# A chunked-attention and channel-mixer kernel on one core: two late tiles turned on TensorE, one batch's halving done in the lead-in, and the slot lists set anew

## The chip, the cores and the metric

The kernel runs on one core of one Trainium2 chip. A core has five engines that run side by side, each taking its own instructions strictly in order: TensorE (PE, with its weight loads as PEld), VectorE (DVE), ScalarE (ACT), GpSimd (POOL) and SyncE (SP, which here only issues transfers). The metric is the device time of one execution in microseconds, from the first to the last instruction and a little around it; lower is better.

## The reference

```python
# attention, within chunks of 64 positions, for 8 batches, 8 heads, 576 positions, head size 64
scores = scale * np.matmul(q_c, k_c.transpose(0, 1, 2, 4, 3))
attn = softmax(scores)                       # row maximum taken off, exp, divided by the sum + 1e-9
x = matmul(attn, v_c)                        # then laid out as [batch, 576, 512]
# mixer
h = x.transpose(0, 2, 1) @ U @ V             # rank 32, along the positions
u = x + h.transpose(0, 2, 1)
out = u + np.maximum(u @ w_ch1, 0.0) @ w_ch2 # 512 -> 2048 -> 512
```

q, k and v are float32; U, V, w_ch1 and w_ch2 are float64 and are rounded to float32 pairs on the chip. The two large products are done in three passes each (high times high, high times low, low times high), which is what makes TensorE the busiest engine.

## The kernel before, in words

The 8 x 576 positions are cut into 36 tiles of 128, T0 to T35; two batches make a pair of nine tiles (T0 to T8, T9 to T17, T18 to T26, T27 to T35). In names, the first number is the pair and the second the tile in it, so `es_8` of pair 1 belongs to T17 and `us_0` to T9. The tiles are taken in ten groups (`GROUPS`, line 55): groups 0 to 2 have three tiles, the others four, but for the last with three. For a group, each of 16 rounds f does `hidden` (line 759: 12 multiplications of the group's turned x+u with one slice of w_ch1 into a PSUM bank), `relu_high` on ACT (line 777) and `relu_low` on DVE (line 782), and `project_out` (line 789: three multiplications for each tile of the group, two with the high half of the relu and one with the low half). A round's `project_out` stands one round later in the program.

Groups 0 and 1 and everything before them, the lead-in, are put in order by a small planner (lines 129 to 211). From group 2 on the order is written by hand in `LISTS` (line 958): one string for a group, each word a step and the slot at which it is recorded. A round has one slot more than the group has tiles. What the loop records there is placed on each engine by the compiler's own scheduler, so order may shift by a few rows. The words: `m` loads a tile's q, k and v; `t` turns q and k; `s` takes scores and exp and sends the result through DRAM; `q` turns the result that came back; `a` multiplies with v; `p` and `y` take x times U; `l` computes x+u; `f` and `u` bring it into its turned form; `w` splits it into a high (ACT, line 735) and a low half (DVE, line 739); `r` fetches x+u again for the end.

From pair 1 on no operand is turned on TensorE. q and k are first halved: `halve` (line 390) copies one batch's q or k within DRAM so that 32 columns stand together; eight such transfers make a batch. Those of batches 2 and 3 are issued by SP in the lead-in (line 889), those of batches 4 to 7 by POOL, one in each of nine of a group's 16 rounds (line 1001), each not before a given `hidden` has run. A tile's x+u goes the same way: `put_u` (line 720) writes it to DRAM with four transfers on SP, `fetch_u` (line 723) reads it back turned by blocks, and `square_u` (line 728) turns the blocks of 32 on DVE. Only pair 0 turns x+u on TensorE (`transposed`, line 714). The columns that a group multiplies are complete only when all its tiles have been split, so the last tiles of a group are wanted before the first `hidden` of that group: T9 to T12 before group 3, T13 to T16 before group 4.

Of the kernel before, what the change touches and what calls it, by code (L numbers as in the profile page):

```python
# [11 lines left out]
F32 = mybir.dt.float32  # L12
# [10 lines left out]
def kernel(  # L23
# [11 lines left out]
    nc = tc.nc  # L35
    B, H, S, D = q.shape
# [3 lines left out]
    DF, DM = moe_w_ch2.shape[0], moe_w_ch1.shape[0]  # L40
    P = 128
# [14 lines left out]
    GROUPS += [[13, 14, 15, 16], [19, 20, 17, 18], [21, 22, 23, 24], [27, 28, 25, 26], [29, 30, 31, 32], [35, 33, 34]]  # L56
    PLACES = [0, 3, 0, 2, 0, 2, 0, 2, 0, 3]
    LATE = {2: [12], 3: [15, 16], 4: [19, 20], 5: [23, 24], 6: [27, 28], 7: [31, 32], 8: [35]}
    BLOCKS = [(hp, e, c) for hp in range(HP) for e in range(2) for c in range(2)]
    NPAIR = B // 2  # L60
    SCALE = 1.0 / float(D) ** 0.5
# [7 lines left out]
    dram = ctx.enter_context(tc.tile_pool(name="dram", bufs=1, space=bass.MemoryType.DRAM))  # L69
# [60 lines left out]
    rank = [0]  # L130
# [252 lines left out]
    x_of = {}  # L383
    y_of = {}
    rest = {}
# [17 lines left out]
    def halvings(b):  # L403
        return [lambda w=w: halve(b, *w) for w in [(z, e, g) for z in range(2) for e in range(2) for g in range(2)]]
# [288 lines left out]
    def mix_ops(pr, t, x, ys, after=None, first=None):  # L693
        n = f"{pr}_{t}"
        st = {}
        T = pr * NT + t
# [17 lines left out]
        def transposed():  # L714
            x = x_of[pr, t]
            st["t"] = pt = bank("ut_" + n)
            for cc in range(NCC):
                nc.tensor.transpose(pt[:, cc * P : (cc + 1) * P], x[:, cc * P : (cc + 1) * P], ident)

        def put_u():  # L720
            st["kept"] = put(x_of[pr, t], "us_" + n, by_channel=True)

        def fetch_u():
            st["us"] = fetch(st["kept"], slot(("us", "uT")[T % 2], F32, "us_" + n, (P, P // SQ, P)))
            rest[pr, t] = dram.tile([P, DM], F32, name="rest_" + n)
            nc.gpsimd.dma_start(rest[pr, t], x_of[pr, t])  # L726

        def square_u():
            uT = st["t"] = slot("eT", F32, "uT_" + n)
# [13 lines left out]
        ad = Op("DVE", 0.69, add, lr, free="bank")  # L743
        if (pr, t) == (0, 0):
            Op("PE", 0.01, end_filling, lr, free="bank")
        if pr > 0:
            pu = Op("SP", 2.0, put_u, ad, lat=2.0)
            fe = Op("SP", 2.0, fetch_u, pu, take="us", lat=2.0)
            tr = Op("DVE", 0.71, square_u, fe, take="uT", free="us")
            hi = Op("ACT", 0.59, high, tr, take="" if j else "ut")  # L750
            lo = Op("DVE", 0.69, low, hi, free="uT")
            return [[lr, ad, pu], [fe], [tr], [hi, lo]]
        tr = Op("PE", 0.55, transposed, ad, take="bank")
        hi = Op("ACT", 0.59, high, tr, first, take="" if j else "ut")
        lo = Op("DVE", 0.69, low, hi, free="bank")
# [131 lines left out]
    prev = None  # L887
    blocks = 0
    second = halvings(2) + halvings(3)
    gates = dict(zip(GATES, range(len(GATES))))  # L890
    for g, f0, f1 in STRETCHES:
        for f in range(f0, f1):
            rank[0] = BASE
            prev = block_ops(g, f, f == 0, f == NF - 1, [*w_done[f], *mixed[g]], prev)
            blocks += 1
            if (g, f) == (0, NF - 1):
                last = prev
            if blocks >= HALVES_FROM and second:
                rank[0] = 0
                Op("SP", 0.6, second.pop(0), prev[0], lat=3.0)  # L900
            if blocks in gates:
                rank[0] = 0
                attention_ops(1, gates[blocks], prev[0])
# [23 lines left out]


    assert not second
    to_halve = [w for b in range(4, B) for w in halvings(b)]  # L930
    pend = None

    def flush(j):
# [20 lines left out]
    def do(group):  # L954
# [1 line left out]
            (o.run if isinstance(o, Op) else o)()  # L956

    LISTS = (
# [8 lines left out]
    )  # L967
# [22 lines left out]
    for g, words in enumerate(LISTS, 2):  # L990
        words = words.split()
        slots = 0
        asked = [z.split("@")[0] for z in words]
        late = [z for T in LATE.get(g, []) for z in (f"u{T}", f"w{T}") if z not in asked]
        width = len(GROUPS[g])
        last = g == len(GROUPS) - 1
        for f in range(NF):
            ps = hidden(g, f)
            hh = relu_high(g, f, ps)
            hs = hh, relu_low(g, f, ps, hh)  # L1000
            if (f % 2 or f == 8) and to_halve:
                to_halve.pop(0)()
            for j in range(width + 1):
                while words and int(words[0].split("@")[1]) <= slots:
                    go(words.pop(0).split("@")[0])
                slots += 1
                if f == NF - 1 and j > 0 and late:
                    go(late.pop(0))
                flush(j)
            pend = g, f, hs  # L1010
        assert not words and not late
        if not last:
            for j in range(width):
                flush(j)
            pend = None
# [34 lines left out]
```

## Time and profile before

| | us |
|---|---|
| median of 3 executions | 959.55 (958.25 to 961.33) |
| profiled execution, whole | 957.67 |
| its span, first to last instruction | 955.9 |
| PE busy | 926.7 |
| DVE, ACT, POOL busy | 485.8, 207.5, 235.9 |

How to read the rows: a line of the timeline gives the start from the beginning of the span, the time taken, the engine, the source line, the operation and its tiles (result on the left of the arrow), how many instructions were merged, and in square brackets how long the engine had been idle before and what ended that wait. For transfers issued by SP or POOL the time is that of issuing, not of the transfer.

### The profile page before, as it was taken

What the parts mean: (1) busy time and instruction counts of PE and PEld (TensorE: products, weight loads), DVE (VectorE), ACT (ScalarE), POOL (GpSimd) and SP (SyncE); (2) the same over time, 40 slices, a digit from 0 to 9 for tenths busy, and PEclk for the clock granted to TensorE, in tenths of its full rate; (3) what the DMA queues carried; (4) which work ended last, traced back from release to release, by engine and by line L of the source; (5) the groups of instructions that cost most, each with busy time, mean ns of one, the idle gap of its engine ahead of it and who ended that gap; (6) DMA issues with size and microseconds to landing.
All of it is one profiled execution on the core that took longest, in us unless ns stands there. A gap on an engine that the chain in (4) does not pass through costs nothing.

```text
span 955.9 us, 15482 instructions
## 1 busy us (share of the span) xinstructions
PE 926.7 (97%) x6258; PEld 761.9 (80%) x6258; DVE 485.8 (51%) x891; ACT 207.5 (22%) x347; POOL 235.9 (25%) x314
## 2 busy tenths in 40 slices
PE   7789999999989999999999999999999999999998
PEld 4559899878877787777777878778778888888997
DVE  6789999975446435643455453553355224211211
ACT  5434333322112121112121211112111111111110
POOL 5410000015645345355344421221211001000000
PEclk9999999999999999999999999999999999999999
DMA  9980698445686446755396454431525035200100
GB/s 216 220 247 1 141 193 167 127 144 129 125 184 165 94 103 145 214 135 127 70 235 158 87 128 134 136 97 57 154 90 143 1 88 143 56 1 1 45 1 33
DMA packets 174103, 113.14 MB, mean 118 GB/s; under 512 B 125872, under 2 KB 149424, under 8 KB 174032
## 3 DMA queue, kind: packets, MB, share of 16 engines
q1 hardware_dynamic: 156256, 66.49, 28.8%
q0 software_dynamic: 17168, 45.52, 20.0%
q8 instruction: 49, 0.80, 0.4%
q14 instruction: 22, 0.18, 0.1%
q10 hardware_dynamic: 608, 0.15, 0.1%
HBM read 80.92 MB, written 44.83 MB: 132 GB/s over the span
## 4 chain that ended last, share of the span: by engine, by line
PE 84%; DMA 8%; DVE 3%; SPq 2%; issue 2%; ACT 1%; POOL 0%; DVEq 0%; ACTq 0%; POOLq 0%
PE o L796 38%; PE h L768 38%; PE av L563 2%; DMA qkv<-in_k_dram 2%; PE sc L515 2%; DMA es_4d<-ex 1%; DMA us_6d<-x 1%; SPq L432 1%; PE u L706 1%; PE y L663 1%; SPq L462 1%; PE y L662 1%; DMA es<-es_4d 1%; DMA us<-us_0d 1%; PE y L669 1%
## 5 line engine op out<-in xcount | busy, mean ns | idle before, releaser
L796 PE MATMUL o<-w,hbuf 128*128 128x512 f32 x1728 | 435.6, 395 | 4.0 <-ACT hbuf L779 4.0
L768 PE MATMUL h<-uth,w 128*128 128x512 f32 (+1 forms) x1280 | 390.2, 370 | 2.0 <-DVE ex L536 1.6
L796 PEld LDWEIGHTS o<-w,hbuf 128*128 128x128 f32 x1728 | 321.5, 188 | 71.8 <-ACT hbuf L779 5.1
L768 PEld LDWEIGHTS h<-uth,w 128*128 128x128 f32 x1280 | 237.9, 188 | 36.4 <-issue 2.0
L768 PE MATMUL h<-utl,w 128*128 128x512 f32 (+1 forms) x640 | 236.1, 369 | 1.3 <-DVE utl L739 1.3
L784 DVE SCALAR_TENSOR_TENSOR hbuf<-h,hbuf 128x512 fp32r<-128x512 f32 (+1 forms) x160 | 100.7, 630 | 209.1 <-ACT hbuf L779 208.3
L779 ACT ACTIVATE hbuf<-h 128x512 fp32r<-128x512 f32 (+1 forms) x160 | 88.8, 556 | 486.0 <-PE h L768 484.4
L768 PEld LDWEIGHTS h<-utl,w 128*128 128x128 f32 x640 | 120.4, 188 | 18.5 <-DVE utl L739 1.6
L446 POOL DMA_DIRECT2D vn<-in_v_dram x96 | 59.8, 632 | 8.0 <-issue 8.0
L421 POOL MEMSET vn<- 128x8 f32 x27 | 3.1, 116 | 209.5 <-DVE w L359 141.8
L425 POOL DMA_DIRECT2D qn<-halfq x24 | 21.5, 895 | 131.5 <-DVE kT L471 123.6
L396 POOL DMA_DIRECT2D halfq<-in_q_dram x16 | 40.7, 2544 | 46.6 <-PE h L768 38.7
L471 DVE STREAM_TRANSPOSE uT<-us 128x512 f32<-128x512 f32 x27 | 29.5, 1092 | 42.7 <-DMA us<-us_0d 10.7
L471 DVE STREAM_TRANSPOSE eT<-es 128x512 f32<-128x512 f32 x27 | 29.1, 1078 | 36.0 <-PE h L768 8.7
L396 POOL DMA_DIRECT2D halfk<-in_k_dram x16 | 40.7, 2546 | 21.5 <-PE h L768 11.3
L544 ACT ACTIVATE ex<-ex 128x512 f32<-128x512 f32 x36 | 22.8, 633 | 92.2 <-DVE ex L536 85.9
L471 DVE STREAM_TRANSPOSE qT<-qn 128x512 f32<-128x512 f32 x27 | 19.2, 712 | 42.2 <-PE h L768 39.0
L726 POOL DMA_DIRECT2D rest<-x x27 | 18.0, 668 | 73.3 <-DVE x L712 72.3
L655 DVE TENSOR_TENSOR xl<-x,xh 128x512 fp32r<-128x512 f32 x30 | 20.6, 686 | 28.6 <-PE y L663 28.4
L529 DVE TENSOR_REDUCE mx<-sc 128x4 f32<-128x256 f32 x72 | 28.1, 412 | 12.3 <-PE sc L515 12.0
L712 DVE TENSOR_TENSOR x<-u,x 128x512 f32<-128x512 f32 x36 | 24.0, 681 | 14.6 <-PE u L706 14.4
L563 PEld LDWEIGHTS av<-vn,eT 64*64 64x64 f32 x864 | 17.8, 133 | 17.0 <-issue 17.0
(95 smaller groups left out, 650.4 us busy)
## 6 DMA issues: line engine op xcount, KB each, us to landing
wraw<-in_moe_w_ch_dram SPq DMA_DIRECT2D x32, 512.0 KB, 6.3
rest<-x POOLq DMA_DIRECT2D x27, 256.0 KB, 3.7
rest<-rest POOLq DMA_DIRECT2D x27, 256.0 KB, 4.7
out_dram<-rest SPq DMA_DIRECT2D x27, 256.0 KB, 2.0
vn<-in_v_dram POOLq DMA_DIRECT2D x96, 64.0 KB, 2.5
qn<-halfq POOLq DMA_DIRECT2D x24, 256.0 KB, 3.9
kn<-halfk POOLq DMA_DIRECT2D x24, 256.0 KB, 3.9
halfq<-in_q_dram POOLq DMA_DIRECT2D x16, 288.0 KB, 7.4
```

What stands on the lines that cost most here:

```text
L396: moved = queue.dma_start(halves[pr, z][odd * n : (odd + 1) * n, 2 * e + g].rearrange("n s (h i) -> n s h i", i=SQ), (q, k)[z][b, e * HP : ...
L425: queue.dma_start(dst.rearrange("p (n a) c -> p n a c", n=2), halves[pr, z][2 * t : 2 * t + 2].rearrange("n x (j a) c -> (x j) n a c", a=2),)
L446: d = queue.dma_start(vn[e * C : (e + 1) * C, c, :, 0:D], v[b, heads(pr, t, e), s0 : s0 + C, :].rearrange("h s d -> s h d"),)
L471: turned = nc.vector.transpose(dst, src)
L529: nc.vector.reduce_max(mx, st["sc"][e], axis=AX.X)
L544: nc.scalar.activation(exf, exf, AF.Exp, scale=SCALE)
L563: nc.tensor.matmul(ps[e][cs, hp * D1 : (hp + 1) * D1], lhsT=st["eT_"][rows, hp, cs], rhs=vn[rows, c, hp, :], start=True, stop=True,)
L712: nc.vector.tensor_add(x, st["u"], x)
L768: o = nc.tensor.matmul(ps[:, :n], lhsT=w[:, z, cc], rhs=ut[u][:, cc, cols], start=(i == 0), stop=(i == 3 * NCC - 1))
L779: nc.scalar.activation(hh, ps[:, 0 : len(GROUPS[g]) * P], AF.Relu)
L784: nc.vector.scalar_tensor_tensor(hl, ps[:, 0 : len(GROUPS[g]) * P], 0.0, hh, op0=ALU.max, op1=ALU.subtract)
L796: nc.tensor.matmul(acc[g, j], lhsT=h[:, js], rhs=w2[f][:, z], start=(first and i == 0), stop=(final and i == 2),)
```

## The change

Four things are edited.

1. For T11 and T12 (`TURNED`) `mix_ops` takes the way of pair 0: after the addition, TensorE turns x+u with four 128 x 128 transposes into a PSUM bank, and ACT and DVE split it from there. Their eight `put_u` transfers, two fetches and two DVE transposes are gone; the write of `rest` (line 725) now comes with the addition.
2. The eight halvings of batch 4 become operations of the lead-in's planner, on POOL, after those of batches 2 and 3.
3. The remaining 24 halvings are issued in six rounds of a group (f = 1, 4, 6, 9, 11, 14) in place of nine.
4. `LISTS` has other slots in groups 2 to 7.

```diff
+    TURNED = (11, 12)
...
+        def put_rest():
+            rest[pr, t] = dram.tile([P, DM], F32, name="rest_" + n)
+            nc.gpsimd.dma_start(rest[pr, t], x_of[pr, t])
...
+        if T in TURNED:
+            tr = Op("PE", 0.55, transposed, ad, take="bank")
+            hi = Op("ACT", 0.59, high, tr)
+            lo = Op("DVE", 0.69, low, hi, free="bank")
+            return [[lr, ad, put_rest], [], [tr], [hi, lo]]
...
+    third = halvings(4)
...
+            elif blocks >= HALVES_FROM and third:
+                rank[0] = 0
+                Op("POOL", 2.6, third.pop(0), prev[0], lat=3.0)
...
-    to_halve = [w for b in range(4, B) for w in halvings(b)]
+    to_halve = [*third, *(w for b in range(5, B) for w in halvings(b))]
...
-            if (f % 2 or f == 8) and to_halve:
+            if f % 5 in (1, 4) and to_halve:
```

Of the lists, the words of group 2 that differ are `u9@50 w9@50 ... u10@52 w10@52 ... u11@55 w11@55 ... u12@59` before and `u9@52 w9@52 u11@53 w11@53 ... u10@55 w10@55 ... u12@58` now. In group 3, `m17`, `m18`, `m19` go from slots 9, 20, 32 to 3, 16, 27, `s17` from 19 to 20, `a17` from 29 to 31, and the steps `l13` to `u14` two or three slots later; in groups 4 to 7 only the loads `m` are recorded earlier, by four to six slots.

On ACT, at the end of group 2 (`h_13`, `h_14`, `h_15` are its last rounds, `h_0` and `h_1` the first of group 3; `uT_0` is T9, `uT_1` T10, and T11 and T12 are `uT_2`, `uT_3` before, `ut_2`, `ut_3` now; `ex_6` is T15's exp), before:

```order
L735 CAST uth<-uT_0_2837 128x4x128
L779 ACTIVATE hbuf<-h_13_2856 128x384
L735 CAST uth<-uT_1_2872 128x4x128
L779 ACTIVATE hbuf<-h_14_2897 128x384
L735 CAST uth<-uT_2_2893 128x4x128
L779 ACTIVATE hbuf<-h_15_2962 128x384
L735 CAST uth<-uT_3_2960 128x4x128
L544 ACTIVATE ex_6_2933<-ex_6_2933 128x512
```

and now:

```order
L787 ACTIVATE hbuf<-h_13_2848 128x384
L738 CAST uth<-uT_0_2863 128x4x128
L738 CAST uth<-ut_2_2870 128x4x128
L738 CAST uth<-uT_1_2887 128x4x128
L787 ACTIVATE hbuf<-h_14_2891 128x384
L545 ACTIVATE ex_6_2928<-ex_6_2928 128x512
L787 ACTIVATE hbuf<-h_15_2960 128x384
L738 CAST uth<-ut_3_2942 128x4x128
```

The relu of round 13 has moved ahead of T9's split; the exp of T15 has moved ahead of the relu of round 15.

On DVE at the same place (`qT_6`, `kT_6` are T15's; `hbuf<-h_13,hbuf` is the low half of round 13's relu), before:

```order
L471 STREAM_TRANSPOSE uT_0_2837<-us_0_2771 128x4x128
L712 TENSOR_TENSOR x_3_2501<-u_3_2841,x_3_2501 128x512
L739 TENSOR_TENSOR utl<-uT_0_2837,uth 128x4x128
L471 STREAM_TRANSPOSE qT_6_2883<-qn_6_2687 128x2x2x4x32
L784 SCALAR_TENSOR_TENSOR hbuf<-h_13_2856,hbuf 128x384
```

and now:

```order
L713 TENSOR_TENSOR x_3_2510<-u_3_2840,x_3_2510 128x512
L472 STREAM_TRANSPOSE uT_0_2863<-us_0_2777 128x4x128
L472 STREAM_TRANSPOSE qT_6_2877<-qn_6_2693 128x2x2x4x32
L792 SCALAR_TENSOR_TENSOR hbuf<-h_13_2848,hbuf 128x384
L472 STREAM_TRANSPOSE kT_6_2879<-kn_6_2694 128x2x2x4x32
```

The low half of round 13 still stands behind the turning of T9's fetched tile; T12's addition has moved ahead of it.

On POOL in the last third of the lead-in (`vn_0` to `vn_2` are the v tiles of T9, T10 and T11; `qkv_7` is T7's), before:

```order
L446 DMA qkv_7_681<-in_v_dram 64x4x64 x4
L421 MEMSET vn_0_1798 128x8
L421 MEMSET vn_1_1895 128x8
L421 MEMSET vn_2_2136 128x8
L421 MEMSET vn_3_2265 128x8
```

and now:

```order
L447 DMA qkv_7_681<-in_v_dram 64x4x64 x4
L397 DMA halfq_1738<-in_q_dram 9x256x32 x2
L422 MEMSET vn_0_1801 128x8
L397 DMA halfq_1738<-in_q_dram 9x256x32 x2
L422 MEMSET vn_1_1900 128x8
L397 DMA halfk_1941<-in_k_dram 9x256x32 x4
L422 MEMSET vn_2_2146 128x8
L422 MEMSET vn_3_2274 128x8
```

Four halvings stand ahead of the fill of `vn_1`, four behind it.

## Rows read from the trace of the kernel before

**Rows 1.** The page, part 1: busy time of each engine, its share of the span and its instructions.

```profile
PE 926.7 (97%) x6258; PEld 761.9 (80%) x6258; DVE 485.8 (51%) x891; ACT 207.5 (22%) x347; POOL 235.9 (25%) x314
```

**Rows 2.** The waits of PE: what it waited for, us in total, times, longest.

```profile
PE o L796 <- ACT hbuf L779: 4.0, 2, 2.8
PE av L563 <- DVE eT L471: 3.8, 3, 2.3
```

**Rows 3.** The timeline of PE at the end of group 2: the last multiplication of the `hidden` of round 14, and the `project_out` of rounds 12 and 13 around it.

```profile
276.27 2.24 PE L796 MATMUL o<-w,hbuf 128*128 128x512 f32 x9
...
280.28 0.34 PE L768 MATMUL h<-uth,w 128*128 128x384 f32 x1
...
283.38 3.91 PE L796 MATMUL o<-w,hbuf 128*128 128x512 f32 x9 [2.75 <-ACT hbuf L779]
```

**Rows 4.** The timeline of ACT there: T9's split and the relu of round 13.

```profile
282.31 0.62 ACT L735 CAST uth<-uT 128x512 fp32r<-128x512 f32 x1 [10.97 <-DVE uT L471]
282.84 0.48 ACT L779 ACTIVATE hbuf<-h 128x384 fp32r<-128x384 f32 x1
```

**Rows 5.** The timeline of DVE there: T9's turning, T15's q, the low half of round 13.

```profile
281.20 1.08 DVE L471 STREAM_TRANSPOSE uT<-us 128x512 f32<-128x512 f32 x1 [6.70 <-DMA us<-us_0d]
...
283.57 0.71 DVE L471 STREAM_TRANSPOSE qT<-qn 128x512 f32<-128x512 f32 x1
284.20 0.52 DVE L784 SCALAR_TENSOR_TENSOR hbuf<-h,hbuf 128x384 fp32r<-128x384 f32 x1
```

**Rows 6.** The timeline of SP there: x+u of T9 (`us_0`), T10 and T11 (`us_2`) written out, T9's and T10's fetched.

```profile
267.15 4.13 SPq L462 DMA_DIRECT2D us_0d<-x  x4
...
274.72 0.50 SPq L407 DMA_DIRECT2D us<-us_0d  x1
275.27 3.75 SPq L462 DMA_DIRECT2D us_2d<-x  x3
279.48 0.33 SPq L407 DMA_DIRECT2D us<-us_1d  x1
```

**Rows 7.** A stretch of 10 us with that place: busy time (and instructions) of PE, PEld, DVE, ACT and POOL, then the granted clock of PE as a share of full speed, the busy share of the DMA engines and GB/s.

```profile
280.00:290.00 10.00, 7.25 (x57) 5.72 (x56) 7.26 (x11) 2.64 (x5) 4.56 (x4) 0.83 0.84 201
```

**Rows 8.** The timeline of PE in the lead-in, where a tile of pair 0 is turned on TensorE and `project_out` follows; and, from the groups by line, ACT's split of such a tile from PSUM (busy us, mean ns).

```profile
198.03 0.66 PE L718 MATMUL ut<-hbuf,x 128*128 128x128 f32 x4
198.44 0.94 PE L796 MATMUL o<-w,hbuf 128*128 128x512 f32 x3
...
L735 ACT CAST uth<-ut 128x512 fp32r<-128x512 f32 x9 | 5.2, 590 | 3.9 <-PE ut L718 3.9
```

**Rows 9.** The timeline of T17 in group 3, on PE, DVE and SP: its scores and its product with v on PE, its row maxima and the turning of its fetched result on DVE, and its result written out and fetched.

```profile
317.76 0.65 PE L515 MATMUL sc<-kT,qT 64*64 64x64 f32 x32
...
331.77 0.81 PE L563 MATMUL av<-vn,eT 64*64 64x65 f32 x32 [2.25 <-DVE eT L471]
...
319.21 0.74 DVE L529 TENSOR_REDUCE mx<-sc 128x4 f32<-128x256 f32 x2
...
330.43 1.08 DVE L471 STREAM_TRANSPOSE eT<-es 128x512 f32<-128x512 f32 x1 [4.70 <-DMA es<-es_8d]
...
321.36 0.37 SPq L467 DMA_DIRECT2D es_8d<-ex  x1
326.21 0.32 SPq L407 DMA_DIRECT2D es<-es_8d  x1
```

**Rows 10.** The timeline at the end of group 3: `project_out` of round 14 on PE, T14's split and the exp ahead of that round's relu on ACT, and T14's fetch on SP.

```profile
393.82 5.78 PE L796 MATMUL o<-w,hbuf 128*128 128x512 f32 x24 [1.22 <-ACT hbuf L779]
...
391.45 0.62 ACT L735 CAST uth<-uT 128x512 fp32r<-128x512 f32 x1 [10.36 <-DVE uT L471]
392.65 0.63 ACT L544 ACTIVATE ex<-ex 128x512 f32<-128x512 f32 x1 [0.58 <-DMA us<-us_6d]
...
383.40 1.54 SPq L407 DMA_DIRECT2D us<-us_5d  x1
```

**Rows 11.** The timeline of PE at the product with v of T13 (group 2) and of T22 (group 4), and a halving that POOL issued while T13's result was on its way.

```profile
256.66 0.70 PE L563 MATMUL av<-vn,eT 64*64 64x65 f32 x32 [0.63 <-DVE eT L471]
...
440.26 0.75 PE L563 MATMUL av<-vn,eT 64*64 64x65 f32 x30 [0.91 <-DVE eT L471]
...
248.22 2.54 POOL L396 DMA_DIRECT2D halfk<-in_k_dram  x1 [0.69 <-PE h L768]
```

**Rows 12.** The timeline of the last third of the lead-in: POOL's fill of `vn_1`, SP's load of T9's k, and T9's k turned on DVE.

```profile
192.52 0.11 POOL L421 MEMSET vn<- 128x8 f32 x1 [141.82 <-DVE w L359]
...
171.53 0.46 SPq L425 DMA_DIRECT2D kn<-halfk  x1
...
180.27 0.71 DVE L471 STREAM_TRANSPOSE kT<-kn 128x512 f32<-128x512 f32 x1
```

**Rows 13.** Two stretches of 5 us there, columns as in rows 7.

```profile
170.00:175.00 5.00, 5.00 (x29) 4.84 (x28) 4.65 (x9) 1.54 (x3) 0.00 (x0) 1.00 0.85 185
175.00:180.00 5.00, 5.00 (x26) 4.46 (x25) 4.81 (x10) 2.19 (x4) 0.00 (x0) 1.00 0.11 24
```

**Rows 14.** The page: POOL's queue with its packets, MB and share of the 16 DMA engines' span; the issue of a q halving on POOL (busy us, mean ns); and its size and time from issue to landing.

```profile
q0 software_dynamic: 17168, 45.52, 20.0%
...
L396 POOL DMA_DIRECT2D halfq<-in_q_dram x16 | 40.7, 2544 | 46.6 <-PE h L768 38.7
...
halfq<-in_q_dram POOLq DMA_DIRECT2D x16, 288.0 KB, 7.4
```

More of the change, by code (lines that the diff above doesn't have):

```diff
@@ L724, in fetch_u @@
             st["us"] = fetch(st["kept"], slot(("us", "uT")[T % 2], F32, "us_" + n, (P, P // SQ, P)))
-            rest[pr, t] = dram.tile([P, DM], F32, name="rest_" + n)
-            nc.gpsimd.dma_start(rest[pr, t], x_of[pr, t])
         def square_u():
@@ L751, in mix_ops @@
             lo = Op("DVE", 0.69, low, hi, free="uT")
-            return [[lr, ad, pu], [fe], [tr], [hi, lo]]
+            return [[lr, ad, pu], [fe, put_rest], [tr], [hi, lo]]
         tr = Op("PE", 0.55, transposed, ad, take="bank")
```

12 rows, old and new, of the table LISTS are left out of this document.

## The prediction

> **What bounds the kernel now.** I read the page's first part before all else: the reader is to see PE busy for 926.7 us of a span of 955.9, and no other engine above 486 [rows 1]. So 29.2 us of PE are idle, and a change that adds no work to PE can win only from these and from time that PE spends at a low clock. Next come the waits of PE [rows 2]. The two that fall behind the lead-in are `project_out` waiting for ACT's relu (4.0 us in two pieces, the longest 2.8) and the product with v waiting for a turned tile from DVE (3.8 us in three). Then I looked each piece up in the timeline, to see what the releasing engine itself had waited for.
>
> The longest is at the end of group 2 [rows 3]. PE has finished the `hidden` of round 14 at 280.28 + 0.34 = 280.62 and starts the `project_out` of round 13 at 283.38, after 2.75 us. The relu it waits for ran on ACT only at 282.84, behind T9's split, for which ACT had been idle 10.97 us [rows 4]. That split waited for DVE's turning of T9, which waited 6.70 us for the transfer `us_0` [rows 5]. SP had issued that fetch at 274.72 and then at once three more writes of T11, 3.75 us of issuing [rows 6]. The wait has a second price. Nine multiplications that took 2.24 us take 3.91 behind it [rows 3], 1.67 us more, and the granted clock of the 10 us around is 0.83 [rows 7]: for a part of that stretch PE ran at 1.2 GHz in place of 2.4. Together 4.42 us.
>
> **The change, part by part.** All terms are against the profiled execution's own 957.67 us, which is 1.9 us below the median of 959.55.
>
> *(a) End of group 2.* The relu of round 13 no longer stands behind T9's split on ACT, so the 4.42 us lose their cause. Added are two tiles turned on TensorE. In the lead-in the next multiplication starts 198.44 - 198.03 = 0.41 us after four such transposes [rows 8], so PE gets 2 x 0.41 = 0.82 us. ACT's split from PSUM takes 0.59 us [rows 8] against 0.62 from SBUF [rows 4]: nothing. What is late next? First, DVE: the low half of round 13 still stands behind T9's turning and T15's q. PE, after the transposes, is through `hidden` at 280.62 + 0.41 = 281.0 and has six multiplications with the high half (6 x 2.24/9 = 1.5 us), so it wants the low half at 282.5. DVE has it 1.08 + 0.71 + 0.52 = 2.3 us after `us_0` lands [rows 5]. If that lands at 281.2 as before, PE waits 1.0 us. But T11's writes, which ran beside the fetch [rows 6], are gone; I take half of their 3.75 us of issuing as gain, so it lands near 279.3 and PE does not wait. Second, the relu of round 15 now stands behind T15's exp on ACT, and the exp behind four DVE operations of the scores: two maxima of 0.74 together [rows 9], two subtractions taken as long, and the exp of 0.63 [rows 10], 2.1 us at most, of which PE's own work covers some: I take 1.0, about the middle, with 0 and 2.1 as ends. T10's fetch, issued at 279.48 behind T11's writes [rows 6], can now go right behind T9's and should not be late. Term (a): -4.42 + 0.82 + 1.0 = -2.6, from -3.6 (nothing late) to -0.5 (both waits in full).
>
> *(b) T17 in group 3.* PE waits 2.25 us for its turned result [rows 9]. The scores move one slot and the product two. By the orders, 48 multiplications stand between them before and 50 now, at 2.24/9 = 0.25 us: 0.5 us more cover. The scores also come behind a `hidden`, so the 319.21 - 317.76 - 0.65 = 0.8 us that DVE let them lie before (it was scaling T16) should go. If the two transfers keep their times (321.36 to 330.43), the wait shrinks by 1.3. I take -1.3; the ends are 0 and -2.25.
>
> *(c) End of group 3.* PE waits 1.22 us for the relu of round 14, which stood on ACT behind T14's split and T18's exp, up to 392.65 + 0.63 [rows 10]. The exp now comes after the relu, and SP issues T14's fetch ahead of T15's writes, no longer at 383.40 behind them. All the additions of that group are two slots later, however, so T16, the last, may become late at the first `hidden` of group 4. I take -1.0, from -1.22 to +0.5.
>
> *(d) T13 and T22.* Waits of 0.63 and 0.91 us for their results [rows 11]. While T13's was on its way POOL issued a halving at 248.22; with six rounds in place of nine that one falls away, and T23's load goes four slots ahead of T22's trip. Nothing in the trace prices a transfer with less beside it, so the bounds are 0 and -1.54; I take half, -0.8.
>
> *(e) The lead-in.* Eight halvings of 2.54 us issue each [rows 14] go on POOL, which did nothing there for 141.82 us [rows 12]: the issuing is hidden. The transfers are not free. POOL's queue moved 45.52 MB in 20.0% of the span [rows 14], 191 us, so 288 KB (0.295 MB) take 1.24 us of all 16 engines, and the four that stand ahead of the fill of `vn_1` 5.0 us. From 170 to 180 the engines were free for 0.15 x 5 + 0.89 x 5 = 5.2 us [rows 13], and T9's k, issued by 171.99, was turned at 180.27 without waiting for it [rows 12]. So they just fit. The other four are issued from 192.52 to about 202.7, beside T10's trip through DRAM and T11's loads. The planner's order on DVE and PE is fixed there, so anything late is paid in full. I take +0.5, with 0 and +2 as ends.
>
> The Trainium skill bears on this place (DMA: Bandwidth & Descriptors, section Queues, rings and completion order): each DMA engine goes in turn through the queues that have work, a packet at a time. By that rule POOL's halvings would not stand ahead of SP's loads but at most double their time, here 0.85 x 5 = 4.25 us of work in 8.5 us, done by about 178.5 and thus before 180.27, at a cost of 0; the sum would be 0.5 lower. The rows do not show the two queues side by side in the lead-in.
>
> *(f)* The remaining list changes move loads earlier, off PE's path; POOL then waits in line longer for a free tile. Behind 500 us PE does not wait at all, and I see no new wait, but take +0.2 for one.
>
> Sum: -2.6 - 1.3 - 1.0 - 0.8 + 0.5 + 0.2 = -5.0. That is 952.7 for a profiled execution, and with the 1.9 us to the median **954.6 us**.
>
> **The rivals.**
>
> *The wait only changes engine.* DVE's order keeps T9's turning ahead of round 13's low half. If `us_0` lands no earlier, (a) is about -0.5, and if transfers keep their times elsewhere too, (d) is 0, (b) half its term and (c) lost at T16. Sum about -0.5 - 0.6 + 0 + 0.5 = -0.6: 957.1 profiled, 959.0. For it: the fetch's 6.5 us [rows 5, 6] hold the loads of T16's v too, which stay. Against it: three of T11's writes lay directly behind the fetch in the same queue.
>
> *All the waits go.* With fewer and thinner transfers every trip is shorter: (a) -3.6, (b) -2.25, (c) -1.22, (d) -1.54, (e) 0. Sum -8.6: 949.1, at the median 951.0. For it: the changed lists move just the loads that lay beside those trips. Against it: T15's exp ahead of a relu.
>
> *Slower: the lead-in's halvings hold up T9.* If the DMA engines serve two halvings whole ahead of T9's k, its turn comes at 171.99 + 2 x 7.4 [rows 14] = 186.8, and with half of the 4.25 us of work of that load and its neighbour it lands at 188.9, 8.6 us behind the 180.27 at which DVE wants it [rows 12]. T9's scores stand in PE's fixed order, so PE waits 8.6 us and pays 1.67 us for the clock as in rows 3. With the other terms, -5.5 + 8.6 + 1.7 = +4.8: 962.5, at the median 964.4. It decides, slower by over 2.9 us, from about 6.7 us late on. For it: the engines were 0.85 busy when T9's loads ran [rows 13]. Against it: by the share above two halvings need 2.5 us of the engines, not 14.8.
>
> **How the numbers follow.** The forecast has 0.60, the wait that changes engine 0.20, all waits gone 0.13, the lead-in 0.07. A difference that this kernel's runs can tell is about 0.3%, 2.9 us: faster means below 956.7. The likeliest case's own range is 952 to 957. The whole one reaches up to the first rival, which ends near 959, and down towards the second, 951; it leaves out the lead-in's rival and a little on either side: 950.5 to 959. Faster: 0.58 of the forecast's 0.60 and all of the second rival, 0.71. Same: the first rival and the rest of the forecast, 0.21. Slower: the lead-in and 0.01 for what I do not see, 0.08.
>
> **What would show it.** In the changed profile: the wait of `project_out` for the relu near 280 gone, and the clock at 1.00 in that stretch (a). If a wait of 1 us stands there with the low half of the relu as its releaser, DVE's order is the cause; if it stands at round 15, T15's exp. The wait at T17 about 1 us (b), that of round 14 in group 3 gone with none at the first `hidden` of group 4 (c), those at T13 and T22 about halved (d). T9's k turned on DVE without a wait for its transfer (e). I am wrong if PE waits longer between 180 and 215 than before, or if a new wait of over 2 us stands in groups 4 to 9.

## The result and the profile after

The changed kernel takes 967.61 us, the median of 15 runs (961.23 to 971.13), beside 960.54 of the kernel before on the same chip: a ratio of 1.0069 [1.0047, 1.0091], slower by 0.7%. (All times are medians; two executions in the experiments below, of 1033.33 and 1025.04 us at a granted clock of 0.85, are left out of them.) Forecast were 954.6 and a range of 950.5 to 959. The profiled execution takes 966.22 us with a span of 964.4, 8.55 us more than the profiled one of before, which was one of that kernel's faster executions.

Part 1 of its page, then the waits of PE from 150 to 900 us (what it waited for, us in total, times, longest), which answer to [rows 1] and [rows 2]:

```profile
PE 931.4 (97%) x6266; PEld 764.6 (79%) x6266; DVE 489.6 (51%) x889; ACT 207.0 (21%) x347; POOL 235.4 (24%) x314
...
PE h L776 <- DVE x L583: 5.2, 2, 4.8
PE o L804 <- DVE hbuf L792: 3.3, 3, 1.8
PE av L564 <- POOL vn L422: 3.1, 1, 3.1
PE h L776 <- DVE ex L537: 2.1, 2, 1.5
PE h L776 <- ACT uth L738: 1.0, 1, 1.0
```

The two lines of [rows 2] are not there any more: no product waits for `eT`, no `project_out` for ACT. Every wait that the prediction meant to shorten in groups 2 to 4 is gone, 7.8 us in five pieces with 1.67 us of clock; a single new one of 1.0 us stands at the first `hidden` of group 4, behind T16's split. But three waits stand where there was none, and they are larger in sum.

**First, 163 to 184 us, in the lead-in.** The timeline of POOL and of DVE in the changed kernel:

```profile
162.85 2.54 POOL L397 DMA_DIRECT2D halfq<-in_q_dram  x1 [111.14 <-PE h L776]
172.82 2.53 POOL L397 DMA_DIRECT2D halfq<-in_q_dram  x1 [7.44 <-issue]
174.48 6.00 POOL L397 DMA_DIRECT2D halfq<-in_q_dram  x2
...
163.17 0.56 DVE L792 SCALAR_TENSOR_TENSOR hbuf<-h,hbuf 128x384 fp32r<-128x384 f32 x1
163.65 1.99 DVE L119 TENSOR_SCALAR wraw<-wroom 128x512 uint32<-128x512 uint32 x1
...
170.20 0.43 DVE L119 TENSOR_SCALAR wraw<-wroom 128x512 uint32<-128x512 uint32 x1
...
173.98 4.21 DVE L119 TENSOR_SCALAR wraw<-wroom 128x512 uint32<-128x512 uint32 x1
```

The same conversion of weights takes 0.43 us alone, 1.99 and 4.21 us when it falls into POOL's issuing of a halving; the first ends at 165.64, when POOL is through (165.39). The second ends at 178.19, just behind the end (177.94) of the first of the two issues in POOL's third row. DVE's low halves of the relu come late behind it, which is the wait of `o` for `hbuf`, 0.46, 1.83 and 1.00 us, and the wait of a `hidden` for DVE's `ex` is 1.5 us in place of 1.1.

**Second, 210 us, T10's product with v.** The changed kernel's timeline of SP and POOL, then of DVE and PE:

```profile
198.86 0.37 SPq L468 DMA_DIRECT2D es_1d<-ex  x1
204.04 0.34 SPq L408 DMA_DIRECT2D es<-es_1d  x1
204.43 2.98 SPq L818 DMA_DIRECT2D out_dram<-x  x3
...
196.36 7.60 POOL L397 DMA_DIRECT2D halfk<-in_k_dram  x3 [0.54 <-PE sc L516]
...
210.93 0.76 DVE L583 TENSOR_TENSOR x<-av,vn 128x256 f32<-128x256 f32 x2 [4.79 <-DMA out_dram<-x]
211.60 1.07 DVE L472 STREAM_TRANSPOSE eT<-es 128x512 f32<-128x512 f32 x1
...
212.78 1.26 PE L564 MATMUL av<-vn,eT 64*64 64x65 f32 x32 [3.06 <-POOL vn L422]
...
214.73 5.00 PE L804 MATMUL o<-w,hbuf 128*128 128x512 f32 x18
```

and the same rows of SP and DVE in the kernel before:

```profile
195.61 0.37 SPq L467 DMA_DIRECT2D es_1d<-ex  x1
197.94 0.34 SPq L407 DMA_DIRECT2D es<-es_1d  x1
200.14 2.72 SPq L810 DMA_DIRECT2D out_dram<-x  x3
...
203.36 0.76 DVE L582 TENSOR_TENSOR x<-av,vn 128x256 f32<-128x256 f32 x2 [0.49 <-DMA out_dram<-x]
```

Three halvings run beside T10's scores on their way to DRAM. From write to fetch pass 5.18 us instead of 2.33. SP works in order, so the three writes of the output behind that fetch are late as well; they free the tiles of x into which DVE scales T9, DVE waits 4.79 us, and the turning of T10's result stands behind that in DVE's order. PE's row names POOL's `vn`, whose fill was done at 195.8; the releaser that came last is DVE's `eT`, which starts only at 211.60. Behind the wait PE runs in part at 1.2 GHz: the product takes 1.26 us, of T13 it took 0.70 [rows 11]; four transposes 1.11 for 0.66 [rows 8]; 18 projections 5.00 for twice 2.24 [rows 3]. That is 1.5 us in all.

**Third, 577 us, the end of group 5.** POOL, SP, DVE and PE of the changed kernel, and two stretches of 5 us (columns as in [rows 7]):

```profile
566.94 2.54 POOL L397 DMA_DIRECT2D halfk<-in_k_dram  x1 [1.08 <-PE h L776]
...
572.77 1.01 SPq L408 DMA_DIRECT2D us<-us_4d  x1
...
580.67 1.08 DVE L472 STREAM_TRANSPOSE uT<-us 128x512 f32<-128x512 f32 x1 [6.84 <-DMA us<-us_4d]
581.61 0.15 DVE L577 RECIPROCAL vn<-vn 128x8 f32<-128x8 f32 x1
581.81 0.76 DVE L583 TENSOR_TENSOR x<-av,vn 128x256 f32<-128x256 f32 x2
...
582.38 0.77 PE L776 MATMUL h<-uth,w 128*128 128x512 f32 x1 [4.82 <-DVE x L583]
...
580.00:585.00 5.00, 2.62 (x6) 2.15 (x7) 3.77 (x9) 1.09 (x2) 1.66 (x4) 0.63 0.68 185
585.00:590.00 5.00, 5.00 (x17) 3.90 (x16) 1.62 (x2) 0.75 (x2) 1.63 (x3) 0.68 0.54 155
```

The last halving, that of round 14, is issued (566.94) just as x+u of three tiles starts on its way through DRAM. `us_4` is turned 7.9 us after its fetch was issued. DVE's scaling of an attention tile stands behind that turning and frees the PSUM tile that the next `hidden` needs. PE waits 4.82 us and then has a granted clock of 0.63 and 0.68. Twelve `hidden` multiplications and twelve of `project_out` behind the wait take 5.26 and 3.16 us, the same numbers of them in group 3 2.75 and 2.88: 2.8 us for the clock.

The balance of the waits against before: first place +3.7, second +3.1 and some 1.5 of clock, third +4.8 and 2.8, two tiles turned +0.8, T16 +1.0, waits and clock that went -9.4. Together +8.3. The starts of the same relu on ACT in both traces are a check on it:

| relu on ACT | before | now | now later by | of it since the row above |
|---|---|---|---|---|
| ahead of the first place | 157.67 | 156.36 | -1.3 | -1.3 |
| behind the first place | 186.69 | 189.94 | 3.3 | 4.6 |
| behind the second | 216.04 | 223.95 | 7.9 | 4.7 |
| ahead of the third, group 5 | 566.06 | 566.74 | 0.7 | -7.2 |
| behind the third | 585.14 | 593.62 | 8.5 | 7.8 |
| the last of the kernel | 947.75 | 956.24 | 8.5 | 0.0 |

In the first row nothing edited has run yet: POOL issues the first of the moved halvings only at 162.85. The first place costs 4.6 us, more than its waits.

### The profile page after: what moved, and what is told of

Same layout as the page of the kernel before. It is cut to its first block, busy times and chain, and to the rows that moved or that the text cites. A ratio compares the mean times of both kernels' runs of the same rounds, so it can differ in the third digit from the quotient of the medians.

```text
span 964.4 us, 15477 instructions
## 1 busy us (share of the span) xinstructions
PE 931.4 (97%) x6266; PEld 764.6 (79%) x6266; DVE 489.6 (51%) x889; ACT 207.0 (21%) x347; POOL 235.4 (24%) x314
## 4 chain that ended last, share of the span: by engine, by line
PE 87%; DVE 4%; DMA 4%; SPq 2%; issue 1%; ACT 1%; POOL 0%; DVEq 0%; ACTq 0%
PE h L776 40%; PE o L804 38%; PE av L564 2%; PE sc L516 2%; DMA qkv<-in_k_dram 1%; DMA us<-us_6d 1%; PE y L670 1%; PE u L707 1%; PE y L664 1%; DMA us<-us_4d 1%; PE y L663 1%; SPq L433 1%; DVE wraw L119 1%; SPq L434 1%; DMA out_dram<-x 1%
## 5 line engine op out<-in xcount | busy, mean ns | idle before, releaser
L472 DVE STREAM_TRANSPOSE uT<-us 128x512 f32<-128x512 f32 x25 | 27.3, 1092 | 40.0 <-PE h L776 10.9
L723 POOL DMA_DIRECT2D rest<-x x27 | 15.3, 565 | 82.4 <-DVE x L713 82.1
L576 DVE TENSOR_SCALAR vn<-av 128x4 f32<-128x4 f32 x54 | 6.3, 156 | 44.7 <-issue 27.4
```

The costliest lines, as they stand in the source:

```text
L472: turned = nc.vector.transpose(dst, src)
```

## The experiments

Beside what each names, the order of instructions on ACT and DVE is that of the kernel it starts from, but for one row on DVE in the first and the fifth; in the seventh and the last the scheduler also set some rows at the end of group 2 otherwise, T15's exp ahead of round 15's relu among them. What else differs is on POOL and SP. Each kernel has one trace. In the first 85 us, which only the last three studies edit, one trace falls 3.2 us behind that of before and another gets 2.5 us ahead, so the traces are read stretch by stretch and the gain or loss is taken from the ratios.

**The changed kernel without the lead-in's halvings, with the rule of before.**

```
-    third = halvings(4)
+    third = []
-            if f % 5 in (1, 4) and to_halve:
+            if (f % 2 or f == 8) and to_halve:
```

> The changed kernel without its lead-in halvings: batch 4 is halved in the groups again, by the rule of before (nine rounds a group). PE, ACT, DVE and SP keep the changed kernel's order; only POOL differs. Theory (the loss is where POOL issues the halvings, the turned tiles and the lists are a gain): the waits of 3.06 us at 209.7 and of 4.82 us at 577.6 and the four at 167 to 187 go, and the gain stays, so about 16 us less than the changed kernel's profile: 950 to 955, ratio to the kernel before 0.990 to 0.996. Rival (the turned tiles or the lists cost, the halvings only stand near): the 3.06 and the 4.82 stay, ratio 1.005 to 1.009.

957.59 us, ratio 0.9955 [0.9934, 0.9977]. The turned tiles and the new lists are a gain of about 4 us by the runs. (The two traces differ by 0.1 us, 955.8 for 955.9, as that of before is of one of its faster executions: 957.67, the median here 961.37.) All three losses are gone. With nine halvings a group, waits remain in groups 2 to 4 (PE, 150 to 900 us):

```profile
PE av L564 <- DVE eT L472: 2.8, 2, 1.7
...
PE av L564 <- issue: 1.1, 1, 1.1
PE o L804 <- DVE hbuf L792: 1.0, 2, 0.7
```

**The kernel before with the lead-in's halvings on POOL, and nothing else.** The other 24 keep the rule of before and end in group 4.

```
+            elif blocks >= HALVES_FROM and third:
+                rank[0] = 0
+                Op("POOL", 2.6, third.pop(0), prev[0], lat=3.0)
```

> The kernel before with one part of the change: batch 4's eight halvings issued by POOL in the lead-in, the other 24 by the rule of before, so that they end in group 4. PE, ACT, DVE and SP keep the order of before; only POOL differs. Theory: the lead-in's loss of the changed kernel comes whole (3.7 us of short waits from 167 to 187, 3.06 us at T10's product and 1.7 us of half clock behind it), and no loss at the end of group 5: 966 to 970, ratio 1.006 to 1.010. Rival (the lists make the loss): ratio 0.998 to 1.002, with no wait over 2 us between 160 and 215 beyond those of before.

970.61 us, ratio 1.0107 [1.0076, 1.0139]: a little above the range expected. The loss comes whole, the waits at the same two places with 3.3 and 3.5 us; followed at the same relus, the first place costs 4.6 us and the second 5.3. The lists have no part in it.

**Only the first four of these eight.**

```
+    third = halvings(4)[:4]
```

> The kernel before with only the four halvings of batch 4's q in the lead-in on POOL (in the last study of the kernel before with a lead-in it was all eight); the other 28 by the rule of before. Theory (two losses in the lead-in, each with its own halvings): the first four still lengthen DVE's 128x512 conversion beside POOL's issues, 3.7 us; the wait at T10's product and its half clock, 4.8 to 5.2 us, belong to the four that follow and go. 963 to 966, ratio 1.002 to 1.006. Rival (one loss, the load on the DMA engines as a whole): both about halved, or both gone with T10's product waiting 1 to 2 us.

966.5 us, ratio 1.0056 [1.0032, 1.0079], at the upper end of what was expected. DVE's conversions are as slow as before with all eight and the wait for `hbuf` is 3.3 us again, while T10's product waits for nothing. So there are two losses, each with its own four halvings, of about 5 us each by the two ratios (each with 2 to 3 us to either side).

**The lead-in's halvings on SP in place of POOL, all else as changed.**

```
-        queue = nc.sync if pr < 2 else nc.gpsimd
+        queue = nc.sync if b < 5 else nc.gpsimd
-                Op("POOL", 2.6, third.pop(0), prev[0], lat=3.0)
+                Op("SP", 0.6, third.pop(0), prev[0], lat=3.0)
```

> The changed kernel with the lead-in's eight halvings issued by SP in place of POOL, at the same places; PE, ACT and DVE keep their order. Theory A (POOL's issuing holds DVE up): DVE's conversion of 128x512 that took 1.99 and 4.21 us beside POOL's issues takes 0.43 again, PE's waits at 178 and 182 go, and with them 3 to 4 us; the wait at T10's product may stay, as the transfers are the same. Ratio 1.000 to 1.005. Theory B (the transfers themselves share the DMA engines with what DVE and PE wait for): DVE's rows as in the changed kernel's trace or the waits at the same places in other operations, ratio 1.005 to 1.010.

966.6 us, ratio 1.0053 [1.0032, 1.0074]. Groups by line on DVE, 150 to 215 us (busy us, mean ns; six conversions of 128x512 and one twice as large), of the changed kernel:

```profile
L119 DVE TENSOR_SCALAR wraw<-wroom 128x512 uint32<-128x512 uint32 (+1 forms) x7 | 8.6, 1225 | 0.2
```

and of this one:

```profile
L119 DVE TENSOR_SCALAR wraw<-wroom 128x512 uint32<-128x512 uint32 (+1 forms) x7 | 3.2, 460 | 0.2
```

The same bytes move at the same places of the program, and the mean is back at 460 ns, that of before, the wait for `hbuf` gone: the first loss comes from the issuer, theory A. But the time hardly falls, and the ratio lies in the range of theory B. T10's product now waits 4.1 us and a `hidden` before it 2.8. SP's loads and trips stand behind and beside its own halvings: T10's fetch is issued 6.4 us after its write, 5.2 with POOL as the issuer and 2.3 before. So the second loss stays with either issuer and belongs to the place; how much of it is the shared DMA engines and how much SP's order, these runs do not separate.

**The remaining 24 by the rule of before, the lead-in as changed.**

```
-            if f % 5 in (1, 4) and to_halve:
+            if (f % 2 or f == 8) and to_halve:
```

> The changed kernel with the lead-in's halvings kept and the remaining 24 spread by the rule of before (nine rounds a group), so that the last is issued in group 4 and none in group 5. Theory (a halving issued beside the trips of x+u at the end of group 5 delays the transfer us_4): the wait of 4.82 us at 577.6 and the 3.4 us of half clock behind it go, the lead-in's loss stays: 957 to 961, ratio 0.997 to 1.001. Rival (the trip is late for another reason, the lists of group 5 or chance): the wait stays at about 5 us, ratio 1.005 to 1.009. A third outcome: the denser halvings bring back a wait of 1 to 2 us in groups 2 or 3.

965.2 us, ratio 1.0047 [1.0027, 1.0066]: above what the theory gave. In the trace the wait at 577 is gone as expected, but the denser halvings bring back others, the third outcome: 2.3 us for T16's split at the first `hidden` of group 4, 1.3 for turned results, 1.5 for relus and their low halves near 290 and 298.

**Group 5's six halvings at rounds 1, 2, 4, 5, 7 and 8.**

```
-            if f % 5 in (1, 4) and to_halve:
+            if f in ((1, 2, 4, 5, 7, 8) if g == 5 else (1, 4, 6, 9, 11, 14)) and to_halve:
```

> The changed kernel with the six halvings of group 5 put at rounds 1, 2, 4, 5, 7 and 8 in place of 1, 4, 6, 9, 11 and 14; all else, the lead-in too, as in the changed kernel, and only POOL's order differs. Theory (the halving of round 14 delays us_4): the wait of 4.82 us at 577.6 and the 3.4 us of half clock behind it go and nothing comes in their place: 958 to 961, ratio 0.997 to 1.000, the lead-in's loss and the gain of the turned tiles about level. Rival (that trip is late for another reason): the wait stays, ratio 1.005 to 1.009.

960.03 us, ratio 1.0000 [0.9979, 1.0022], 7.6 us below the changed kernel (6.6 by the two ratios), as much as 4.8 and 2.8 of the third place. SP's fetch and DVE's turning of `us_4`, in this kernel:

```profile
572.24 0.37 SPq L408 DMA_DIRECT2D us<-us_4d  x1
...
575.13 1.11 DVE L472 STREAM_TRANSPOSE uT<-us 128x512 f32<-128x512 f32 x1 [0.29 <-DMA us<-us_4d]
```

2.9 us from issue to use in place of 7.9. Only POOL's order was changed, so group 5's late halvings were the cause; that of round 14 is the one beside this fetch.

**The two tiles turned on TensorE alone, in the kernel before.**

```
+    TURNED = (11, 12)
```

> The kernel before with only the two tiles turned on TensorE: lists, halvings and their rule as before. Theory (the turning itself is a gain, the lists add the rest): the wait of 2.75 us at 280.6 and its 1.67 us of clock go, 0.82 us is added; the waits at T17 (2.25), round 14 of group 3 (1.22) and T22 (0.91) stay: 957 to 959.5, ratio 0.996 to 0.999. Rival (the wait only changes engine, DVE's low half behind T9's turning): a wait of 1 to 3 us stays near 281 with DVE as its releaser, ratio 0.999 to 1.001.

960.5 us, ratio 0.9991 [0.9970, 1.0012]: no gain, the rival's time, though ACT is the releaser and not DVE. The trace is of the slowest of its twelve executions, 963.17 us. Its rows at the end of group 2, ACT, DVE and PE:

```profile
280.72 0.62 ACT L738 CAST uth<-uT 128x512 fp32r<-128x512 f32 x1 [11.89 <-DVE uT L472]
281.25 0.48 ACT L787 ACTIVATE hbuf<-h 128x384 fp32r<-128x384 f32 x1
...
279.61 1.08 DVE L472 STREAM_TRANSPOSE uT<-us 128x512 f32<-128x512 f32 x1 [7.62 <-DMA us<-us_0d]
...
278.21 0.34 PE L776 MATMUL h<-uth,w 128*128 128x384 f32 x1
281.79 1.70 PE L804 MATMUL o<-w,hbuf 128*128 128x512 f32 x6 [3.24 <-ACT hbuf L787]
```

`us_0` comes 1.1 us behind the end of that `hidden` (279.61 against 278.55); before it was 0.6 [rows 3, 5]. So T11's missing writes have hardly hastened it, and by the old list the relu still stands behind T9's split on ACT. At round 14 of group 3, where the wait was expected to stay at 1.22 us, the relu keeps PE waiting for 3.71.

**All 24 halvings of the lead-in on SP, two a block from the third block on, group 5 early.**

```
-    HALVES_FROM = 8
+    HALVES_FROM = 3
+            for _ in range(2 if blocks < 8 else 1):
+                if blocks >= HALVES_FROM and (second or third):
+                    Op("SP", 0.6, (second or third).pop(0), prev[0], lat=3.0)
```

> The changed kernel with all 24 of the lead-in's halvings issued by SP, two a block from the third block on (before the change 16, one a block from the eighth), so that the last is out before T9's loads, into the stretch from 70 to 95 us in which the DMA engines of the kernel before stood at 0.00; group 5's halvings at rounds 1, 2, 4, 5, 7 and 8. Theory (the lead-in's losses come from the issuer and from the place beside T9's and T10's transfers, not from the bytes): no wait at 167 to 183 and none at T10's product, none at the end of group 5, the gain of the turned tiles and lists stays: 950 to 954, ratio 0.989 to 0.994. Rival (more bytes in the lead-in cost wherever they stand, as they hold up the weights): waits for the weights between 70 and 180, ratio 0.998 to 1.006.

967.55 us, ratio 1.0075 [1.0048, 1.0102]: the rival, a little above its range. From 130 us on all is as the theory has it, no wait above 1.1 us. But the halvings stand ahead of weights loads in SP's order and wait there for their block:

```profile
79.92 3.35 SPq L397 DMA_DIRECT2D halfq<-in_q_dram  x2
83.51 2.74 SPq L334 DMA_DIRECT2D wraw<-in_moe_w_ch_dram  x1
...
98.83 2.73 SPq L334 DMA_DIRECT2D wraw<-in_moe_w_ch_dram  x1
...
100.00:105.00 5.00, 0.73 (x4) 0.26 (x2) 0.36 (x1) 0.00 (x0) 0.00 (x0) 0.99 0.92 216
105.00:110.00 5.00, 2.01 (x5) 1.63 (x6) 2.03 (x3) 1.81 (x3) 0.00 (x0) 0.50 0.83 137
```

These are the sixth and the seventh load of weights; in the kernel before they went out at 50.50 and 59.79, so they are 33 and 39 us late. PE waits 7.25 us at 100 and 4.69 at 118 and runs at 1.2 GHz behind both.

**Batch 2's halvings without a wait behind two weights loads, batches 3 and 4 in the sixteen old places, group 5 early.**

```
+            for _ in range({4: 6, 5: 2}.get(f, 0)):
+                unheld.pop(0)()
-    second = halvings(2) + halvings(3)
-    third = halvings(4)
+    second = halvings(3) + halvings(4)
```

> The changed kernel with the lead-in's eight extra halvings where they delay nothing that I know of: batch 2's eight on SP without a wait for a block, six right behind the fifth weights load at about 65 us and two behind the sixth, into the stretch in which the DMA engines of the kernel before stood at 0.00; batches 3 and 4 then take the sixteen places on SP that batches 2 and 3 had; nothing on POOL in the lead-in; group 5's halvings at rounds 1, 2, 4, 5, 7 and 8. PE, ACT and DVE keep the order of the changed kernel. Theory (both losses come from issuer, queue and place, none from the turned tiles, the lists or the bytes): no wait over 1.1 us between 95 and 230 and none over 1.1 us behind it, 950 to 954, ratio 0.989 to 0.994. Rival (the earlier halvings hold up the sixth or seventh weights as in the study with two a block): a wait of 3 to 8 us near 110, ratio 0.997 to 1.004.

949.9 us, ratio 0.9897 [0.9864, 0.9929]: faster than both kernels. (The fifth load of weights goes out at 48.83 us, not at 65, and SP issued the first of these halvings at 49.79.) The waits of PE from 150 to 900 us, all of them:

```profile
PE h L780 <- DVE ex L541: 1.7, 2, 1.1
PE u L711 <- DVE x L717: 0.8, 1, 0.8
PE h L780 <- ACT uth L742: 0.6, 1, 0.6
PE h L780 <- DVE x L587: 0.4, 1, 0.4
```

So none of the parts of the change is bad in itself: turned tiles, lists, an earlier halving of batch 4 and the thinner spread all stand in this kernel.

**The same places for the halvings, with the old lists and no tile turned on TensorE.**

> The kernel before with the halvings alone rearranged as in the study beside this one (batch 2 behind the fifth and sixth weights, batches 3 and 4 in the old sixteen places, the other 24 six a group, early in group 5), with the old lists and without tiles turned on TensorE. Theory (turned tiles, lists and thin spreading are worth about 4 us for the first two and some more for the third): the wait near 280 stays at 2 to 3 us, those at T13, T17 and T22 get shorter by half: 956 to 959, ratio 0.995 to 0.999. Rival (the thin spreading alone makes the gain): 950 to 954 as beside it. The other rival (spreading is worth nothing): ratio 0.999 to 1.001.

952.88 us, ratio 0.9923 [0.9899, 0.9947]: the rival by which the spreading alone makes the gain has it. The waits for turned results at T13, T17 and T22 are gone without any list changed, and so is the wait near 280, which was expected to stay: `us_0` is turned at 275.93, 3.3 us after its fetch was issued at 272.59, and the `project_out` behind T9's split waits 0.27 us. Another wait stands 11 us later. PE, DVE and ACT there:

```profile
278.14 1.66 PE L800 MATMUL o<-w,hbuf 128*128 128x512 f32 x6 [0.27 <-ACT hbuf L783]
289.65 2.93 PE L800 MATMUL o<-w,hbuf 128*128 128x512 f32 x6 [3.19 <-ACT hbuf L783]
...
286.27 1.08 DVE L475 STREAM_TRANSPOSE uT<-us 128x512 f32<-128x512 f32 x1 [1.03 <-DMA us<-us_3d]
...
288.59 0.63 ACT L548 ACTIVATE ex<-ex 128x512 f32<-128x512 f32 x1 [4.07 <-DVE ex L540]
289.13 0.47 ACT L783 ACTIVATE hbuf<-h 128x384 fp32r<-128x384 f32 x1
```

This is the relu of round 15 behind T15's exp, and the exp behind the turning of T12, which waits for its transfer: an order that the scheduler made here and that the kernel before does not have.

What hastens `us_0` can be read across all twelve traces. In the six with nine halvings a group, POOL issues one 3.6 to 5.1 us ahead of the fetch of `us_0`, and 5.9 to 7.2 us pass from the fetch's issue to the turning. In the six with the thin spread there is none in the 11 us ahead of it, and 2.6 to 3.4 us pass. The fifth study differs from the changed kernel in this spread alone: 6.4 against 2.6. T11's writes matter little beside it: with them 6.5 to 7.2 and 3.3 us, without them 5.9 to 6.4 and 2.6 to 3.1.

Placed well, the thin spread is most of the gain by the medians. What turned tiles and lists add, 949.9 against 952.88, is not settled: the two intervals overlap, and the trace has the wait of 3.19 us and a granted clock of 0.50 behind it (290 to 295 us), in an order of the scheduler's, for it.

## Why the prediction was wrong

**(e) is the step that failed first: "the issuing is hidden".** I had taken it from POOL's idle 141.82 us [rows 12], as if an idle issuer cost nobody anything. The change to SP shows that it costs DVE, which is busy for 4.65 and 4.81 of 5 us there [rows 13] and stands between the relu and `project_out`. The Trainium skill has the rule (SBUF — State Buffer, section Who interferes with whom): GpSimd and VectorE share a pair of ports as an exclusive lock, tensor_scalar is among the operations that can take it, and whichever starts first makes the other wait. The trace agrees with the lock: the TENSOR_SCALAR is held, 4.21 us in place of 0.43, and the SCALAR_TENSOR_TENSOR beside the same issue took its usual 0.56. The prediction weighed only the queues. The runs show that it is POOL's issuing; that the issuing of a transfer holds these ports is inferred from the skill's rule, and no run here measured a port apart.

**The other half of (e), four halvings beside T10's trip, had the right worry and the wrong size.** "Anything late is paid in full" is what happened, but the 0.5 us of the sum (0 to 2) stood for 3.1 and 1.5 of clock. I had followed T10's trip alone, and not what lay behind its fetch in SP's order: three output writes, and behind these DVE's scaling and turning. The two halves together, +0.5 in the sum, came to 8.3 us of waits and clock, 9.3 by the relus.

**(f) failed as badly: "behind 500 us PE does not wait at all, and I see no new wait".** The spread of six a group carries the last halvings to rounds 9, 11 and 14 of group 5, beside `us_4`, where before none stood. The sum had 0.2 us for it; it was 7.6, and moving these issues to earlier rounds takes it back. Both signs that the prediction named against itself came: longer waits between 180 and 215, and a new one of over 2 us in groups 4 to 9.

**The gains were rather larger than forecast, and partly for another reason.** (a) The wait near 280 and its clock went, with neither of the two late candidates in its place. But the argument, T11's missing writes hastening `us_0` by 1.9 us, fell: with the turning alone 5.9 us pass from its fetch to its use, 6.5 before, and the wait is 3.24 us. What hastened it is the halving that the thin spread no longer puts ahead of that fetch; (a) did not have it. Either half of the change does nearly all of this: with the new list and the dense spread (first study) 0.70 us of wait are left there, with the thin spread and the old list (last study) 0.27 and 0.71. The second late candidate, T15's exp ahead of round 15's relu, shows in the last study alone, with 3.19 us. (d) came out at its far end, 1.54 us, by the thinner spread, of which I had counted one halving near T13: with the lists and the dense spread T13 and T22 still wait 1.74 and 1.05 us. (b) too came out at its far end, 2.25 us. There the lists with the dense spread and the spread without the lists each take the whole wait away, so the step that I gave, the scores moved by a slot or two, is one of two causes that suffice. The same holds for (c), near its upper end with -0.2 for -1.0: the wait of round 14 is gone in both studies, and T16 is late at the first `hidden` of group 4, as the step had warned, by 1.0 us. Together -9.4 + 1.0 + 0.8 = -7.6 for (a) to (d), where the sum had -5.7; the rival by which all the waits go was right for these groups.

**The rivals.** The first, by which the wait only changes engine, met neither case: in the changed kernel the wait is gone, and with the turning alone it stays with ACT. The slower one was named for the lead-in, at 964.4 us and a chance of 0.07. Its place and sign were right and its mechanism was not: T9's k took 3.8 us from issue to landing, 3.4 before, and was turned at 184.11 without a wait for it. For that load the rule of the Trainium skill that the prediction weighed (DMA: Bandwidth & Descriptors, section Queues, rings and completion order) gave the right cost, 0; for T10's trip, 2.33 to 5.18 us beside three halvings, twice the time, 4.66, would have been a little short. The slower rival met the time roughly because two things that it did not hold, POOL's issuing and group 5, filled its sum.

## What to carry to other kernels

An idle engine is not a free place to issue DMAs from: see which operations of its neighbours run there, and try another issuer before another place. For every transfer that is moved, list what is behind it in the in-order queue and which trip through DRAM runs beside it at the new place, the last one of a series above all; a stretch with a DMA share of 0.00 is the place to look for, provided that nothing in the queue has to wait there. When a series is spread thinner, its tail moves: look up where it ends. And when several edits stand together, run each alone before another gets the credit.

## What the runs showed that was not expected

- DVE's TENSOR_SCALAR of 128x512 takes 0.43 us, and 1.99 and 4.21 us while POOL issues halvings of 2.54 us each, ending 0.25 us behind the end of an issue both times; with SP as the issuer it keeps its 0.43.
- SP's issue of one halving took 0.77 us at 141.21 in the study with two a block, of two at once 3.35 us (79.92) to 6.46 (92.12).
- Each wait of PE of 3 us or more behind the first 60 us, in all of these kernels, was followed by a stretch at 1.2 GHz, which cost 1.5 and 2.8 us in the two places where it is worked out above. Of the shorter ones some were, 2.75 us before and 1.74 us in the first study (a granted clock of 0.50 from 260 to 262 us), and some not, 2.25 us at T17 before (1.00 from 331 to 341).
- With one halving issued 3.6 to 5.1 us ahead of it, the fetch of T9's x+u takes 5.9 to 7.2 us from issue to use, without it 2.6 to 3.4.
